# Where the softmax division happens in a top-32 attention with FFN, and how the weights reach their turned layout

## The chip, the cores and the metric

The kernel runs on one core of a Trainium2 chip. The metric is the time of one execution on the device, in microseconds. The time before is the median of three runs, 1543.8 us (1543.63 to 1544.71).

A core has five engines that run their own instruction streams in order: TensorE (PE; its weight loads are shown apart as PEld), VectorE (DVE), ScalarE (ACT), GpSimd (POOL) and SyncE (SP), which here only issues DMAs.

## The reference

```python
# q, k, v: (8, 8, 576, 64); w_in: (512, 2048); w_out: (2048, 512); all float32
scores = q @ k.T / 8
kth = 32nd largest of each row of scores
attn = exp(where(scores >= kth, scores, -1e9) - max)
attn = attn / (sum(attn) + 1e-9)
x = (attn @ v), heads put side by side: (4608, 512)
h = x @ w_in
out = (h - tanh(h)) @ w_out
```

So there is an attention in which each query keeps only its 32 best keys, and a feed-forward layer (FFN) on the result.

## The kernel before, in words

The work is cut into 144 steps. A step is one tile of 128 queries for one pair of heads (`hp`) of one batch `b`; z, the matrix of weights of a step, has 128 rows and 2 x 576 columns. Of the 576 queries of a batch four tiles of 128 are taken in pairs (`nq = 2`), and the last 64 of two head pairs make one step of remainders (`rem`, L-number names below are lines of the kernel). Batch 0 is treated in its own way (`pe`): its weights are turned by TensorE. The steps of batches 1 to 7 are 126: 56 pairs of query tiles and 14 remainders.

A step passes these stages, spread over five steps of a software pipeline written out by hand in `run`:

- `scores` (L237): matmuls into the one PSUM tile for scores, then a ScalarE copy to SBUF (L245).
- `search` (L267 to L278): VectorE finds the 32 largest of each row: a minimum and a maximum of the two halves (L267, L268), then four rounds of MAX8 and MATCH_REPLACE8. After each round, `between(i)` may place other VectorE work.
- `mask` (L294 to L314): GpSimd makes the threshold tb, ScalarE a penalty (L307), GpSimd subtracts it (L310).
- `expo` (L330): ScalarE takes the exponential and sums it; GpSimd adds the epsilon (L340) to give rd.
- `invert` (L345): for the last step of a pair, one VectorE reciprocal of the sums, rd.
- `turn_z` (L376): VectorE turns z within 32 x 32 blocks into zx. In the kernel before this stands in `between(0)`, after the first round of the search two steps later.
- `spread_keys` (L390): the blocks still have to move between the four groups of 32 partitions. Sixteen DMAs, one for each pair of groups, copy zx to et.
- `values` (L433): TensorE multiplies the turned weights with v. Because the weights have not been divided by their sums, the kernel repeats each 1/sum 64 times on GpSimd (L355, rx), turns this with a TensorE transpose (L441), copies product and turned sums out of PSUM (L445, xs), and multiplies the two on GpSimd (L457, L448) to give xT, the input of the FFN.
- `ffn_h` (L486, L498 to L500) and `ffn_o` (L507, L517, L519): the FFN. Its matmuls are the largest part of TensorE's work. They are not a stage of their own: `deal` hands them out in small items between the other instructions of a step, at a rate that `rate` plans from what is waiting and what is to come.

In step n of the loop, the instructions are placed in this order: values of step n-4 (if it is the last of its pair), mask of n-1, search of n with what `between` puts in, spread_keys of n-2, a share of the FFN items, scores of n+1, exponentials of n-1, and more FFN items. As every engine runs in order, this order is also what waits behind what.

Tiles that matter: zx has two buffers, et has one, z has two.

Of the kernel before, what the change touches and what calls it, by code (L numbers as in the profile page):

```python
# [8 lines left out]
AF = mybir.ActivationFunctionType  # L9
ALU = mybir.AluOpType  # L10
FP32 = mybir.dt.float32
# [37 lines left out]
def kernel(  # L49
# [9 lines left out]
    nc = tc.nc  # L59
    P = nc.NUM_PARTITIONS  # L60
# [4 lines left out]
    R = S - JP  # L65
    S2 = S // 2
    N = 2 * P
    CD = DM // P
    CF = DFF // P
    G = 32  # L70
    NG = P // G
    KC = 2 * S // P
    G = 32
    NG = P // G
    WJ = 4
    FJ = CF // WJ
    scale = 1.0 / float(D) ** 0.5
# [5 lines left out]
    def pool(name, bufs, **kw):  # L83
        return ctx.enter_context(tc.tile_pool(name=name, bufs=bufs, **kw))
# [10 lines left out]
    xrpool = pool("xr", 1)  # L95
    thpool = pool("th", 4)
    gpool = pool("g", 4)
    sc_ps = pool("sc_ps", 1, space=PS)
    zt_ps = pool("zt_ps", 2, space=PS)
    h_ps = pool("h_ps", 2, space=PS)  # L100

    ident = consts.tile([P, P], FP32, name="ident")
# [80 lines left out]
    def half(t):  # L183
        return slice(t * D, (t + 1) * D)
# [4 lines left out]
    def load_rows(name, b, hp, exact):  # L189
# [6 lines left out]
        src = {"k": k, "q": q}[name]  # L196
        for a in range(NG):
            h, d = 2 * hp + a // 2, a % 2 * G
            queue = nc.scalar if a and (name, b, hp, exact) == ("q", 0, 0, False) else nc.sync
            queue.dma_start(  # L200
                x[a * G : (a + 1) * G, :].rearrange("i (n d) -> i n d", d=G),
                src[b, h, :, d : d + G].rearrange("(n i) d -> i n d", i=G),
            )
# [22 lines left out]
    st = {}  # L226
# [97 lines left out]
    rds = {}  # L324
# [15 lines left out]
        nc.gpsimd.tensor_scalar(rd[:, g.i, :], den[:], EPS, None, ALU.add)  # L340

    def invert(n):
        if steps[n].last:
            rd = rds[n][:, 0 : steps[n].nq, :]
            nc.vector.reciprocal(rd, rd)  # L345

    rxs = {}

    def spread(n):

        if steps[n].last:
            rd = rds.pop(n)
            nq = steps[n].nq
            rx = rxs[n] = xpool.tile([P, 2, 2, D], FP32, tag="rx", name="rx")
            nc.gpsimd.tensor_copy(  # L355
                rx[:, 0:nq], rd[:, 0:nq].unsqueeze(3).to_broadcast([P, nq, 2, D])
            )
# [3 lines left out]
    def group(a):  # L361
        return slice(a * G, (a + 1) * G)

    def tiles(x, nq):

        x = x[:, 0 : nq * 2 * S]
        return x.rearrange("p (a k i j) -> p a k i j", a=NG, k=KC, j=G)

    def turn_z(n):


        g, z = steps[n], st.pop(n)["z"]
        if g.i == 0:
            last_zx[0] ^= 1
        zx = zxs[n] = zxs.pop(n - 1) if g.i else zx2[last_zx[0]]
        nc.vector.transpose(  # L376
            tiles(zx, g.nq)[:, :, :, g.i, :].rearrange("p c k j -> p k c j"),
            z[:].rearrange("p (k c j) -> p k c j", c=NG, j=G),
        )

    def spread_keys(n):


        zx = zxs.pop(n)
        rem = steps[n].rem
        et = ets[n] = et_rem if rem else etpool.tile([P, 4 * S], FP32, tag="et", name="et")
        w = steps[n].nq * S // 2
        for a in range(NG):
            for c in range(NG):
                nc.sync.dma_start(  # L390
                    et[group(c), a * w : (a + 1) * w], zx[group(a), c * w : (c + 1) * w]
                )

    def turn_pe(n):

# [9 lines left out]
        for k0 in range(0, KC, J):  # L405
# [10 lines left out]
            if k0:  # L416
                yield

    def values(n):

        g = steps[n]
        nq, u = g.nq, g.unit
        et = tiles(ets.pop(n), nq)
        rx = rxs.pop(n)
        w = nq * P
        av = zt_ps.tile([P, 2, N], FP32, tag="zt", name="av")
        for i in range(2 if g.rem else 1):
            cols = half(i) if g.rem else slice(0, w)
            es = et[:, 2 * i : 2 * i + 2] if g.rem else et
            hp = g.hp + i  # L430
            for c in range(J + 1):
                for t in range(2):
                    nc.tensor.matmul(  # L433
                        av[half(t), 0, cols],
                        vb[g.b, hp][:, t, c, :] if c < J else vr[g.b, hp][:, t, :],
                        es[:, :, (J + 1) * t + c if c < J else J].rearrange("p a i j -> p a (i j)"),
                        start=(c == 0),
                        stop=(c == J),
                    )
        for i in range(nq):  # L440
            nc.tensor.transpose(  # L441
                av[:, 1, 0:w].rearrange("p (a i j) -> p i a j", a=NG, i=nq)[:, i], rx[:, i].rearrange("p t d -> p (t d)"), ident[:]
            )
        xs = xrpool.tile([P, 2, N], FP32, tag="xs", name="xs")
        nc.scalar.copy(xs[:, :, 0:w], av[:, :, 0:w])  # L445
        if g.rem:
            for i in range(2):
                nc.gpsimd.tensor_tensor(  # L448
                    xt(u)[:, g.hp + i, g.col : g.col + R],
                    xs[:, 0, half(i)],  # L450
                    xs[:, 1, half(i)],
                    ALU.mult,
                )
        else:

            xv = xs[:, :, 0:w].rearrange("p s (a i j) -> p s i a j", a=NG, i=nq)
            nc.gpsimd.tensor_tensor(  # L457
                xt(u)[:, g.hp, g.col : g.col + w].rearrange("p (i a j) -> p i a j", a=NG, i=nq),
                xv[:, 0],
                xv[:, 1],  # L460
                ALU.mult,
            )
        if n in done:
            work.extend(ffn(u))

# [2 lines left out]
    def xt(u):  # L468
        if u.xT is None:
            p = xpool if u.tag == "xT" else xrpool  # L470
            u.xT = p.tile([P, CD, N], FP32, tag=u.tag, name=u.tag)
        return u.xT
# [48 lines left out]
    def ffn(u):  # L521

        nh = CF * u.n // (2 * P)
        for item in range(nh):
            f = (item + 1) * CF // nh - 1
            yield CD * (f // FJ + 1), u, lambda item=item: ffn_h(u, item)
        for i in range(len(u.blocks)):
            for part in range(CF // 2):
                yield CD * (WJ + part // 2 + 1), None, lambda i=i, part=part: ffn_o(u, i, part)
# [3 lines left out]
    steps, done, work = [], {}, []  # L533
# [36 lines left out]
    def run(exact):  # L570
# [9 lines left out]
        for i, (b, hp) in enumerate(pairs):  # L580
            n = next(n for n, g in enumerate(steps) if (g.b, g.hp) == (b, hp))
# [56 lines left out]
        def here(i):  # L638
            return 0 <= n + i < NS

        def between(i):
            for fn in at_round.pop((n, i), []):
                fn()
            if i == 0 and here(-2):
                invert(n - 2)
                if not steps[n - 2].pe:
                    turn_z(n - 2)


        ready, begun = {}, {}  # L650
# [31 lines left out]
        def deal(part):  # L682
            nonlocal credit
            credit += part * share
            while work and credit > 0 and work[0][0] <= usable:
                work.pop(0)[2]()
                credit -= 1
            credit = min(credit, 1.0)

        for n in range(-4, NS + 4):  # L690
            pe = here(-2) and steps[n - 2].pe
            if here(-3) and not steps[n - 3].pe:
                spread(n - 3)
            for m in (n - 4, n - 3):
                if 0 <= m < NS and steps[m].last and steps[m].lag == n - m:
                    values(m)
            share, usable = rate(), converted[0]
            if pe:
                w = turn_pe(n - 2)
                next(w)  # L700
            if here(-1):
                mask(n - 1, exact)
            if here(0):
                search(n, exact, between)
            elif here(-2):
                between(0)
            if here(-2) and not pe and steps[n - 2].last:
                spread_keys(n - 2)
            if pe:
                spread(n - 2)  # L710
            deal(0.0 if pe else 0.4)
            if here(1):
                scores(n + 1)
            if pe:
                next(w)
            if here(-1):
                expo(n - 1)
            deal(0.8 if pe else 0.2)
            if pe and steps[n - 2].last:
                values(n - 2)  # L720
            deal(0.0 if pe else 0.2)
            for fn in todo.pop(n, []):
                fn()
            deal(0.2)
# [4 lines left out]
    with tc.manual_schedule():  # L729
        run(False)  # L730
# [10 lines left out]
    with tc.If(again > 0):  # L741
        with tc.manual_schedule():
            run(True)
# [29 lines left out]
```

## Time and profile before

| | busy us | share of the span of 1542.8 us |
|---|---|---|
| TensorE, matmuls | 1440.7 | 93% |
| VectorE | 1347.2 | 87% |
| GpSimd | 940.8 | 61% |
| ScalarE | 883.9 | 57% |
| DMA queue q1 | - | 38.5% of 16 engines |

The rows that the change touches, from the groups of instructions (line, engine, count, busy time, mean of one):

| what | count | busy us | mean ns |
|---|---|---|---|
| L441 PE transposes of the repeated sums | 144 | 35.2 | 313 |
| L355 POOL repeats the sums | 84 | 30.8 | 367 |
| L445 ACT copies xs | 84 | 44.2 | 526 |
| L457 and L448 POOL multiply into xT | 100 | 56.8 | 695 and 321 |
| L345 DVE reciprocals | 84 | 14.0 | 167 |
| L376 DVE turns z | 126 instructions | 171.5 | 1361 |
| L390 DMAs zx to et | 1120 | 2.0 us each to landing | |

Busy time is the union of the intervals in which an engine ran such an instruction. Instructions of one engine overlap a little, so the mean of one times the count can exceed it. The idle time that a view shows ahead of an instruction is put down to the semaphore that came last.

### The profile page before, as it was taken

To read this page: it belongs to the slowest core of one execution; us is meant where nothing else is said; L and a number is where in the kernel's file an instruction comes from. 1 tells how busy PE (TensorE), PEld (TensorE's weight loads), DVE (VectorE), ACT (ScalarE), POOL (GpSimd) and SP (SyncE) were. 2 spreads that over 40 slices of the span, in tenths; PEclk is the share of its full clock that TensorE was granted. 3 is DMA by queue.
4 is the path that set the end of the run, shared out by engine and by line. 5 is a ranking of instruction groups with operands and counts; after the bars stand their busy time and mean duration, and the time that the engine had idled before them with its cause. 6 is when DMAs were issued, how large, how long until landed. Compare 5 with 4: busy or idle time off the path is not lost.

```text
span 1542.8 us, 25300 instructions
## 1 busy us (share of the span) xinstructions
PE 1440.7 (93%) x7428; PEld 912.1 (59%) x7428; DVE 1347.2 (87%) x3828; ACT 883.9 (57%) x1567; POOL 940.8 (61%) x1525
## 2 busy tenths in 40 slices
PE   2567899999999999999999999999999999999997
PEld 1355566465666666656566665656566665656673
DVE  6998899999999999999999999999999999997300
ACT  4887776566555565556555565556555565655320
POOL 2777677567665665756565675757565675746420
PEclk9887999999999999999999999999999999999999
DMA  9944113324533354234433354234433344322200
GB/s 241 360 169 168 50 32 76 78 71 102 112 86 80 76 112 101 70 79 95 106 87 79 77 110 103 70 78 96 102 89 79 77 103 109 78 67 58 73 8 16
DMA packets 258835, 147.42 MB, mean 96 GB/s; under 512 B 210048, under 2 KB 217216, under 8 KB 258688
## 3 DMA queue, kind: packets, MB, share of 16 engines
q1 hardware_dynamic: 256912, 145.49, 38.5%
q8 instruction: 62, 1.02, 0.3%
q14 instruction: 85, 0.70, 0.1%
q10 hardware_dynamic: 1776, 0.22, 0.1%
HBM read 61.85 MB, written 9.44 MB: 46 GB/s over the span
## 4 chain that ended last, share of the span: by engine, by line
PE 73%; DVE 10%; SPq 5%; ACT 4%; DMA 2%; issue 2%; POOL 2%; DVEq 0%; ACTq 0%; POOLq 0%
PE ops L507 28%; PE hps L486 26%; PE av L433 9%; PE scps L237 8%; SPq L390 3%; DVE m L275 2%; DVE ab L278 2%; PE av L441 2%; SPq L200 2%; DMA zx<-in_moe_w_in_dram 1%; DVE spare L376 1%; PE zt L409 1%; DVE ab L267 1%; DVE ab L270 1%; DVE ab L268 1%
## 5 line engine op out<-in xcount | busy, mean ns | idle before, releaser
L507 PE MATMUL ops<-w_out,g 128*128 128x512 f32 x1152 | 520.5, 598 | 0.0
L486 PE MATMUL hps<-xT,w_in 128*128 128x256 f32 (+1 forms) x2176 | 471.4, 372 | 1.2 <-POOL xT L457 1.2
L275 DVE MAX8 m<-ab 128x8 f32<-128x288 f32 (+1 forms) x1152 | 465.8, 447 | 0.0
L310 POOL TENSOR_TENSOR z<-sc,z 128x576 f32<-128x576 f32 x288 | 400.2, 1411 | 77.4 <-ACT z L307 77.4
L486 PEld LDWEIGHTS hps<-xT,w_in 128*128 128x128 f32 x2176 | 390.7, 193 | 73.9 <-issue 23.4
L278 DVE MATCH_REPLACE8 ab<-m,ab 128x288 f32<-128x288 f32 x864 | 377.3, 446 | 0.0
L507 PEld LDWEIGHTS ops<-w_out,g 128*128 128x128 f32 x1152 | 211.4, 191 | 244.8 <-issue 240.7
L307 ACT ACTIVATE z<-sc,tb 128x576 f32<-128x576 f32 x288 | 207.6, 769 | 153.1 <-POOL tb L294 153.1
L500 POOL TENSOR_TENSOR g<-g,th 128x512 f32<-128x512 f32 x144 | 183.7, 1276 | 123.5 <-ACT g L499 113.2
L330 ACT ACTIVATE z<-z,nb 128x576 f32<-128x576 f32 x288 | 221.6, 773 | 8.8 <-POOL z L310 8.7
L245 ACT COPY sc<-scps 128x1152 f32<-128x1152 f32 x144 | 160.9, 1117 | 108.5 <-PE scps L237 106.5
L237 PE MATMUL scps<-kT,qT 64*128 64x288 f32 (+1 forms) x1280 | 188.1, 445 | 31.7 <-DVE qT L222 28.1
L237 PEld LDWEIGHTS scps<-kT,qT 64*128 64x128 f32 (+1 forms) x1280 | 101.6, 184 | 120.5 <-issue 60.5
L267 DVE TENSOR_TENSOR ab<-scps,sc 128x576 f32<-128x576 f32 x144 | 108.0, 750 | 69.3 <-POOL bad L314 54.1
L433 PE MATMUL av<-et,vb 128*64 128x256 f32 (+1 forms) x1088 | 131.8, 378 | 37.2 <-ACT et L412 30.4
L457 POOL TENSOR_TENSOR xT<-xs 128x256 f32<-128x256 f32 (+1 forms) x68 | 47.2, 695 | 166.8 <-ACT xs L445 166.8
L498 ACT ACTIVATE th<-hps 128x512 f32<-128x512 f32 x144 | 85.4, 593 | 106.6 <-PE hps L486 104.1
L445 ACT COPY xs<-av 128x512 f32<-128x512 f32 (+1 forms) x84 | 44.2, 526 | 170.2 <-PE av L441 170.2
L433 PEld LDWEIGHTS av<-et,vb 128*64 128x64 f32 x1088 | 75.2, 139 | 98.6 <-ACT et L412 32.5
L340 POOL TENSOR_SCALAR rd<-den 128x2 f32<-128x2 f32 x144 | 33.4, 232 | 140.5 <-ACT z L330 98.2
L270 DVE MAX8 ab<-ab 128x8 f32<-128x288 f32 x288 | 116.9, 448 | 0.0
L268 DVE TENSOR_TENSOR ab<-scps,sc 128x576 f32<-128x576 f32 x144 | 107.8, 749 | 0.0
(67 smaller groups left out, 1253.9 us busy)
## 6 DMA issues: line engine op xcount, KB each, us to landing
et<-spare SPq DMA_DIRECT2D x448, 72.0 KB, 2.0
et<-zx SPq DMA_DIRECT2D x448, 72.0 KB, 2.0
kin<-in_k_dram SPq DMA_DIRECT2D x116, 72.0 KB, 2.4
vb<-in_v_dram SPq DMA_DIRECT2D x64, 128.0 KB, 2.5
out_dram<-ot SPq DMA_DIRECT2D x32, 256.0 KB, 2.2
qin<-in_q_dram SPq DMA_DIRECT2D x113, 72.0 KB, 2.3
w_out<-in_moe_w_in_dram SPq DMA_DIRECT2D x10, 512.0 KB, 5.3
w_out<-in_moe_w_in_dram SPq DMA_DIRECT2D x10, 511.5 KB, 6.1
```

Source lines behind the costliest of these rows:

```text
L237: nc.tensor.matmul(ps[rows, t, s, 0:S2], qT[g.b, g.hp + i][half(t), qs], kT[g.b, g.hp + i][half(t), ks], start=True, stop=True,)
L245: nc.scalar.copy(sc[:], ps[:, :, :, 0:S2])
L270: nc.vector.max(ab[:, t, S2 : S2 + 8], lo[:, t, :])
L275: nc.vector.max(m[:, t, m8], last[t] if i == rounds - 1 else cur[t])
L278: nc.vector.match_replace(nxt[t], m[:, t, m8], cur[t], NEG)
L307: nc.scalar.activation(zv[:, t, :], scf[:, t, :], AF.Relu, bias=tb[:, t : t + 1], scale=-BIG)
L310: nc.gpsimd.tensor_tensor(zv[:, t, :], scf[:, t, :], zv[:, t, :], ALU.subtract)
L330: nc.scalar.activation(x["zv"][:, t, :], x["zv"][:, t, :], AF.Exp, bias=x["nb"][:, t : t + 1], scale=scale, accum_out=den[:, t : t + 1],)
L433: nc.tensor.matmul(av[half(t), 0, cols], vb[g.b, hp][:, t, c, :] if c < J else vr[g.b, hp][:, t, :], es[:, :, (J + 1) * t + c if c < J els ...
L486: nc.tensor.matmul(cur[u][:, s : s + w], w_in[j][:, c, fo : fo + P], u.xT[:, c, 0:w], start=(c == 0), stop=(c == CD - 1),)
L500: nc.gpsimd.tensor_tensor(g, g, th[:], ALU.subtract)
L507: nc.tensor.matmul(cur[u][:], u.g[o // 1024][:, o % 1024 // 512, o % 512 : o % 512 + P], w_out[f // FJ][:, f % FJ, :], start=(f == 0), sto ...
```

## The change

The weights of batches 1 to 7 are divided by their sums before they are turned, by ScalarE (`divide`, two activations with a scale for each row). So the product with v is already the attention output: the repeated sums, their transposes, the copy xs and the GpSimd multiply are gone for these steps, and ScalarE copies the product from PSUM straight into xT. The reciprocal is now taken in each step, and the turning of z moves from after the first round of the search to after the third (`LATE = 2`), so that ScalarE has time for the division.

The sixteen copies between partition groups become one write of all of zx to a scratch tensor in DRAM (two buffers) and four reads, each of which collects the parts for one group of 32 partitions. The write of a pair is 1.18 MB, and the four reads are as much together.

```diff
+    LATE = 2
+    dpool = pool("d", 2, space=bass.MemoryType.DRAM)
     def invert(n):
-        if steps[n].last:
-            rd = rds[n][:, 0 : steps[n].nq, :]
+        g = steps[n]
+        if g.last and g.pe:
+            rd = rds[n][:, 0 : g.nq, :]
             nc.vector.reciprocal(rd, rd)
+        elif not g.pe:
+            rd = rds[n]
+            nc.vector.reciprocal(rd[:, g.i, :], rd[:, g.i, :])
+
+    def divide(n):
+
+        g = steps[n]
+        for t in range(2):
+            x = st[n]["zv"][:, t, :]
+            nc.scalar.activation(x, x, AF.Copy, scale=rds[n][:, g.i, t : t + 1])
+        if g.last:
+            rds.pop(n)
...
         w = steps[n].nq * S // 2
-        for a in range(NG):
-            for c in range(NG):
-                nc.sync.dma_start(
-                    et[group(c), a * w : (a + 1) * w], zx[group(a), c * w : (c + 1) * w]
-                )
+        there = dpool.tile([P, NG * w], FP32, tag=f"there{steps[n].nq}", name="there")
+        nc.sync.dma_start(there[:], zx[:, 0 : NG * w])
+        for c in range(NG):
+            nc.sync.dma_start(
+                et[group(c), 0 : NG * w].rearrange("i (a x) -> i a x", a=NG),
+                there[:, c * w : (c + 1) * w].rearrange("(a i) x -> i a x", a=NG),
+            )
...
-        for i in range(nq):
-            nc.tensor.transpose(
-                av[:, 1, 0:w].rearrange("p (a i j) -> p i a j", a=NG, i=nq)[:, i], rx[:, i].rearrange("p t d -> p (t d)"), ident[:]
-            )
-        xs = xrpool.tile([P, 2, N], FP32, tag="xs", name="xs")
-        nc.scalar.copy(xs[:, :, 0:w], av[:, :, 0:w])
+        if g.pe:
...
+        def put(dst, order, cols):
+            if g.pe:
+                nc.gpsimd.tensor_tensor(dst, order(xs[:, 0, cols]), order(xs[:, 1, cols]), ALU.mult)
+            else:
+                nc.scalar.copy(dst, order(av[:, 0, cols]))
...
             if i == 0 and here(-2):
                 invert(n - 2)
                 if not steps[n - 2].pe:
-                    turn_z(n - 2)
+                    divide(n - 2)
+            if i == LATE and here(-2) and not steps[n - 2].pe:
+                turn_z(n - 2)
...
         for n in range(-4, NS + 4):
             pe = here(-2) and steps[n - 2].pe
-            if here(-3) and not steps[n - 3].pe:
-                spread(n - 3)
```

More of the change, by code (lines that the diff above doesn't have):

```diff
@@ L72 @@
     KC = 2 * S // P
-    G = 32
-    NG = P // G
+    LATE = 2
     WJ = 4
@@ L417, in turn_pe, with in_order @@
                 yield
+    def in_order(x, nq):
+        return x.rearrange("p (a i j) -> p i a j", a=NG, i=nq)
     def values(n):
@@ L423, in values @@
         et = tiles(ets.pop(n), nq)
-        rx = rxs.pop(n)
         w = nq * P
@@ L439, in values @@
                     )
-        for i in range(nq):
-            nc.tensor.transpose(
-                av[:, 1, 0:w].rearrange("p (a i j) -> p i a j", a=NG, i=nq)[:, i], rx[:, i].rearrange("p t d -> p (t d)"), ident[:]
-            )
-        xs = xrpool.tile([P, 2, N], FP32, tag="xs", name="xs")
-        nc.scalar.copy(xs[:, :, 0:w], av[:, :, 0:w])
+        if g.pe:
+            rx = rxs.pop(n)
+            for i in range(nq):
+                nc.tensor.transpose(
+                    in_order(av[:, 1, 0:w], nq)[:, i], rx[:, i].rearrange("p t d -> p (t d)"), ident[:]
+                )
+            xs = xrpool.tile([P, 2, N], FP32, tag="xs", name="xs")
+            nc.scalar.copy(xs[:, :, 0:w], av[:, :, 0:w])
+        def put(dst, order, cols):
[3 more added lines that the diff above has]
+                nc.scalar.copy(dst, order(av[:, 0, cols]))
         if g.rem:
             for i in range(2):
[L448 to L453, printed above, removed]
-        else:
[L456 to L462, printed above, removed]
+                put(xt(u)[:, g.hp + i, g.col : g.col + R], lambda x: x, half(i))
+        else:
+            dst = xt(u)[:, g.hp, g.col : g.col + w].rearrange("p (i a j) -> p i a j", a=NG, i=nq)
+            put(dst, lambda x: in_order(x, nq), slice(0, w))
         if n in done:
@@ L706, in run @@
                 between(0)
+                between(LATE)
             if here(-2) and not pe and steps[n - 2].last:
```

## The prediction

> **What bounds the kernel now.** I read the page's busy shares first, then the windows view from 400 to 1400 us, the groups of instructions, the waits, and the timeline of three steps.
>
> ```profile
> PE 1440.7 (93%) x7428; PEld 912.1 (59%) x7428; DVE 1347.2 (87%) x3828; ACT 883.9 (57%) x1567; POOL 940.8 (61%) x1525
> ...
> 600.00:800.00 200.00, 199.40 (x989) 127.52 (x988) 190.22 (x542) 118.64 (x208) 131.61 (x214) 1.00 0.40 91
> 800.00:1000.00 200.00, 200.00 (x1034) 124.50 (x1033) 189.28 (x538) 114.11 (x203) 126.16 (x213) 1.00 0.37 84
> ```
>
> The columns of the windows are PE, PEld, DVE, ACT and POOL. From about 400 us TensorE has no gap (200.00 of 200 us, at full clock). [...]512-column passes follow each other at 0.43 us for runs of 16. VectorE is 95% busy and waits:
>
> ```profile
> DVE ab L267 <- POOL bad L314: 44.1, 51, 4.4
> DVE ab L267 <- ACT sc L245: 8.8, 9, 1.9
> ```
>
> The first line names GpSimd, but the timeline shows the true end of that wait:
>
> ```profile
> 801.02 0.76 DVE L267 TENSOR_TENSOR ab<-scps,sc 128x576 f32<-128x576 f32 x1 [0.80 <-POOL bad L314]
> 801.83 1.95 PE L433 MATMUL av<-et,vb 128*64 128x256 f32 x16
> 804.14 0.44 PE L441 MATMUL av<-ident,rx 128*128 128x128 f32 x2
> 804.41 3.60 PE L507 MATMUL ops<-w_out,g 128*128 128x512 f32 x8
> 804.65 0.17 DVE L345 RECIPROCAL rd<-rd 128x4 f32<-128x4 f32 x1
> 804.74 1.35 DVE L376 STREAM_TRANSPOSE spare<-z 128x1152 f32<-128x1152 f32 x1
> 806.15 10.28 SPq L390 DMA_DIRECT2D et<-spare  x16
> 806.33 1.44 ACT L307 ACTIVATE z<-sc,tb 128x576 f32<-128x576 f32 x2 [1.13 <-POOL tb L294]
> 807.94 1.24 PE L237 MATMUL scps<-kT,qT 64*128 64x288 f32 x8
> 809.28 1.12 ACT L245 COPY sc<-scps 128x1152 f32<-128x1152 f32 x1 [1.51 <-PE scps L237]
> 810.55 0.76 DVE L267 TENSOR_TENSOR ab<-scps,sc 128x576 f32<-128x576 f32 x1 [0.60 <-POOL bad L314]
> ```
>
> VectorE restarts 0.15 us after the score copy (L245) ends; GpSimd's work had ended long before. The copy waits for score matmuls, which stand in TensorE's order behind the values and dealt FFN matmuls. So TensorE sets the pace: 9.65 us a step (L267 starts at 636.50 and, 40 steps on, at 1022.47), while a VectorE step without a wait takes about 8.8 us. The exception is 250 to 400 us, where VectorE is 99% busy and TensorE 93 to 96%.
>
> [...]in the packet records 2304 B into 32 partitions takes 167 ns (13.8 GB/s per engine, 221 for 16), while 2048 B of an output write from all 128 partitions takes 85 ns (24 GB/s, 386 for 16).
>
> **The change, part by part.** Steps of batches 1 to 7 (126 of 144, 56 pairs of query tiles and 14 remainders) change; batch 0 keeps its way.
>
> *TensorE.* 126 transposes (L441) go. Busy time would say 126/144 of 35.2 us, 30.8 us, but matmuls overlap. By starts, two take 804.14 to 804.41, 0.27 us; one alone 0.17. Summed over the 126 from first start to next other start: 17.7 us. At the very end the FFN waits for the chain transposes, copy, multiply, xT; one scaled copy out of PSUM in place of that saves some 0.3 + 0.7 + 0.2 = 1.2 us. Nothing is added on TensorE. Full realization: 1543.8 - 18.9 = 1525.
>
> *VectorE.* A reciprocal per step instead of per pair: 56 more, 0.08 us from start to next start, 0.17 if nothing overlaps: 5 to 9 us. From 400 us on, VectorE's waits (44.1 + 8.8 us in 1000) hide it; in the 20 steps before, it is paid (1.6 us), and there the transposes' 2.8 us aren't gained either.
>
> *ScalarE.* 252 divisions of 576 elements, 0.77 us: 194 us more, two in each step (1.54 us). It loses the 512-wide xs copies (0.59) for 256-wide ones (about 0.38). Busy goes from 57% to about 70%. Do they delay anyone? They stand after L307 and before the FFN's tanh and the score copy. In an FFN-output step ScalarE idles 1.51 us just there (809.28 above), and L307 itself starts about 1.5 us sooner because its threshold no longer queues on GpSimd behind the xT multiply (L457). In the other kind, with tanh and copy between, TensorE's first half of FFN work (3.6 us after the values) covers L307 plus divisions (0.4 + 1.44 + 1.54). I cost them at nothing for the score copy, but the transpose of z (L376) now waits for them: VectorE reaches it 6.8 us after L267, divisions end about 6.6 to 7.5 us after it, so 0 to 0.7 us of wait in some steps, inside VectorE's slack of 0.5 us a step.
>
> *GpSimd* loses rx and the multiplies, about 31 + 57 us less the part of batch 0; it is off the path.
>
> *The way through DRAM.* This is the risk. The transpose moves two rounds later: it ended 5.05 us after L267, now at 6.8 + 1.37 = 8.2, so 3.15 later. Before, 16 copies took 9.5 to 10.3 us to issue and 2.0 to land: 12 us. Now one write of 1.18 MB, then, after its landing, four reads. The write: 73.7 KB per engine at 24 GB/s is 3.05 us, plus 1.4 (a 256 KB output lands in 2.05, of which 0.68 is data): 4.45 (estimate). The reads: 32 packets per engine at 167 ns is 5.3 us, at 90 ns (what 4096 B in 159 ns scales to) 2.9[...]. Sum 9.4 to 11.8. I take the upper end, since the reads fill 32 partitions each. The values matmuls come 14.9 to 16.2 us after the old transposes' end (820.98 - 806.1), so the data must land 3.15 + 11.8 = 14.95 after it: just in time.
>
> As a loop over four steps: landing; values to VectorE's restart 8.72 - 0.27 = 8.45; a VectorE step 8.87; 8.2 to the end of the transposes; 0.4 for key and query transposes, shared out: 26.0 + L. TensorE's own four steps are 38.6 - 0.56 = 38.0, so L may be 12.0 before the loop binds. Behind these reads on SyncE's queue stand k, q, v loads and output stores; the write's landing blocks them 4.5 us, but the queue is then free after 7 us instead of 10.
>
> *Sum.* 1525, plus 4.4 us for the VectorE-bound stretch, plus about 4 us of late landings and late divisions (L is within 0.3 us of the bound, steps differ by up to 1 us, and only some of that is elastic): 1533.
>
> **Rivals.** (a) Everything hides, L near 10: 1525 + 4 = 1529, down to 1524. For it: the loop's margin would be 2 us. (b) The DRAM round trip sets the pace: L of 12.5 makes the loop 38.5/4 = 9.63, no gain; L of 13.0 gives 9.75, 0.1 us a step more than before over 126 steps, and the early stretch some 5 us: 1543.8 + 13 + 5, near 1560, slower. For it: [...]write traffic to DRAM that the trace shows only in 256 KB pieces, and other loads on the same engines; against: 16 issues of 0.6 us go. (c) Divisions hold VectorE: if the transposes wait 0.7 us in half of the steps with slack already spent, some 126 x 0.5 x 0.25 = 16 us come back and the time stays at about 1543. For it: ScalarE runs in order and its tanh waits for TensorE (L498, 104 us in all). Against: idle time before L245.
>
> **How the numbers follow.** My forecast 0.40 (1530 to 1540), (a) 0.25, (c) and mild forms of (b) 0.13, (b) 0.22. Faster by over 0.2% (under 1540.7) is the first two and a little: 0.65; same 0.12; slower 0.23. The range reaches from (a) to most of (b): 1524 to 1553.
>
> **What would show it.** Right: L441 down to 18 or so transposes, TensorE still over 99% busy from 450 us, step 9.5 us, DRAM write landing about 4.5 us and last read about 11.8 us after the write's issue. Wrong: "PE av <- DMA et" waits of over 20 us (rival b), VectorE waiting on z L356 before its transposes for over 40 us (rival c), or an L of 10 with waits none (a).

## The result and the profile after

The changed kernel takes 1565.7 us against 1544.3 us: 1.0137 times as long (95% interval 1.0122 to 1.0152). The forecast was 1533, faster; it is slower by 21 us. (The time before is here the median of four runs; 1543.8 was that of the first three.)

The page of the changed kernel, in the same columns as before: busy time and share of each engine, two groups of instructions with the idle time ahead of them, and the DMAs with their size and time to landing.

```profile
PE 1436.2 (92%) x7302; PEld 912.5 (58%) x7302; DVE 1353.4 (86%) x3884; ACT 1029.3 (66%) x1833; POOL 869.6 (56%) x1371
...
L356 ACT ACTIVATE z<-z,rd 128x576 f32<-128x576 f32 x252 | 180.1, 763 | 12.9 <-DVE rd L349 12.3
...
L389 DVE STREAM_TRANSPOSE zx<-z 128x1152 f32<-128x1152 f32 x63 | 86.6, 1374 | 35.1 <-ACT z L356 34.9
...
et<-there SPq DMA_DIRECT2D x224, 288.0 KB, 5.3
there<-spare SPq DMA_DIRECT2D x28, 1152.0 KB, 4.2
```

The parts cost what was put down for them: a division 763 ns (0.77 us was put down; L307, an activation of the same shape, has a mean of 769 ns before), the write to DRAM 4.2 us. What is new is idle time. VectorE now waits for the division ahead of L389, the transposes of z; both halves of that group (zx and spare, the two buffers; the remainders' et lies in spare too) together wait 67.8 us, where before it was 4.1. TensorE has lost its closed row, as the windows view shows (columns PE, PEld, DVE, ACT, POOL, clock, DMA share, GB/s):

```profile
600.00:800.00 200.00, 196.27 (x988) 125.45 (x987) 189.95 (x550) 139.53 (x250) 117.16 (x188) 1.00 0.57 147
800.00:1000.00 200.00, 194.66 (x991) 122.65 (x991) 185.58 (x532) 135.32 (x241) 113.67 (x183) 0.99 0.56 145
```

From 400 to 1400 us TensorE was busy 997.1 us before and 975.3 now. The waits view of that stretch (us in total, times, longest) names what it stands for: the values matmuls (L452 now) and the data that they need. Their two PE lines are 23.0 of the 24.7 us that TensorE is idle; before, its waits for these data came to 1.5 us.

```profile
DVE zx L389 <- ACT z L356: 21.4, 23, 3.2
DVE spare L389 <- ACT z L356: 21.0, 22, 3.7
PE av L452 <- DMA et<-there: 18.7, 20, 2.9
PE av L452 <- issue: 4.3, 5, 1.6
```

Two steps of the timeline, with other rows left out, show both waits:

```profile
800.70 1.37 DVE L389 STREAM_TRANSPOSE zx<-z 128x1152 f32<-128x1152 f32 x1
...
802.10 0.34 SPq L402 DMA_DIRECT2D there<-zx  x1
...
803.39 0.76 DVE L267 TENSOR_TENSOR ab<-scps,sc 128x576 f32<-128x576 f32 x1 [0.60 <-ACT sc L245]
...
806.33 2.10 SPq L404 DMA_DIRECT2D et<-there  x4
...
806.96 1.27 POOL L517 TENSOR_TENSOR g<-g,th 128x512 f32<-128x512 f32 x1 [1.83 <-ACT g L516]
807.02 0.16 DVE L349 RECIPROCAL rd<-rd 128x2 f32<-128x2 f32 x1
808.22 0.56 POOL L294 TENSOR_SCALAR tb<-m 128x1 f32<-128x1 f32 x2
...
808.55 1.44 ACT L307 ACTIVATE z<-sc,tb 128x576 f32<-128x576 f32 x2 [1.67 <-POOL tb L294]
...
809.89 1.43 ACT L356 ACTIVATE z<-z,rd 128x576 f32<-128x576 f32 x2
...
811.35 1.38 DVE L389 STREAM_TRANSPOSE spare<-z 128x1152 f32<-128x1152 f32 x1 [1.04 <-ACT z L356]
...
814.43 1.95 PE L452 MATMUL av<-et,vb 128*64 128x256 f32 x16 [0.43 <-DMA et<-there]
...
820.37 1.24 PE L237 MATMUL scps<-kT,qT 64*128 64x288 f32 x8
821.54 7.13 PE L524 MATMUL ops<-w_out,g 128*128 128x512 f32 x16
...
821.66 1.12 ACT L245 COPY sc<-scps 128x1152 f32<-128x1152 f32 x1 [1.77 <-PE scps L237]
...
822.88 0.76 DVE L267 TENSOR_TENSOR ab<-scps,sc 128x576 f32<-128x576 f32 x1 [0.61 <-ACT sc L245]
```

The reciprocal is there at 807.2, but the division begins at 809.89, because L307 stands ahead of it on ScalarE, L307 waits for the threshold, and the threshold queues on GpSimd behind the FFN's subtraction. And the values matmuls at 814.43 wait for a landing: their transposes ended at 802.07, the write went out at 802.10 and the reads from 806.33. The scores behind them, and so VectorE's restart at 822.88, are late by as much, 0.43 us here and up to 2.9 elsewhere. The transposes at 811.35 belong to a later pair; their lateness goes into VectorE's step at once.

From the starts in the traces: from the end of a pair's transposes to its values matmuls it is 15.2 us in the median before. After, it is 12.16 us with a least of 11.88, and 50 of the 56 pairs lie under 12.9. The last copy landed 11.8 us after the transposes before, the last read lands 12.0 us after them now (medians). So before, the data lay there for 3.2 us until TensorE came to them; now the values matmuls start as the data land. The step (starts of L267, steps 42 to 138) went from 9.64 to 9.83 us, and steps 20 to 42, where VectorE had been the bound, from 9.18 to 9.67.

### The profile page after: what moved, and what is told of

Read it like the earlier page. It is cut to its first block, busy times and chain, and to the rows that moved or that the text cites. A ratio compares the mean times of both kernels' runs of the same rounds, so it can differ in the third digit from the quotient of the medians.

```text
span 1565.0 us, 24008 instructions
## 1 busy us (share of the span) xinstructions
PE 1436.2 (92%) x7302; PEld 912.5 (58%) x7302; DVE 1353.4 (86%) x3884; ACT 1029.3 (66%) x1833; POOL 869.6 (56%) x1371
## 4 chain that ended last, share of the span: by engine, by line
PE 45%; DMA 19%; DVE 16%; ACT 9%; issue 4%; SPq 4%; POOL 3%; DVEq 0%; ACTq 0%; POOLq 0%
PE ops L524 16%; PE hps L503 15%; DMA et<-there 11%; PE av L452 8%; DMA there<-zx 5%; DVE m L275 5%; PE scps L237 4%; DVE ab L278 4%; DMA there<-spare 3%; ACT z L307 2%; ACT z L356 2%; SPq L404 2%; POOL g L517 1%; SPq L200 1%; DVE ab L270 1%
## 5 line engine op out<-in xcount | busy, mean ns | idle before, releaser
L517 POOL TENSOR_TENSOR g<-g,th 128x512 f32<-128x512 f32 x144 | 183.5, 1275 | 152.1 <-ACT g L516 147.0
L307 ACT ACTIVATE z<-sc,tb 128x576 f32<-128x576 f32 x288 | 207.6, 770 | 73.8 <-POOL tb L294 73.3
L452 PE MATMUL av<-et,vb 128*64 128x256 f32 (+1 forms) x1088 | 136.4, 387 | 70.9 <-DMA et<-there 33.3
L356 ACT ACTIVATE z<-z,rd 128x576 f32<-128x576 f32 x252 | 180.1, 763 | 12.9 <-DVE rd L349 12.3
L452 PEld LDWEIGHTS av<-et,vb 128*64 128x64 f32 x1088 | 83.7, 142 | 129.8 <-issue 66.9
L267 DVE TENSOR_TENSOR ab<-scps,sc 128x576 f32<-128x576 f32 x144 | 107.0, 743 | 31.2 <-ACT sc L245 24.3
L389 DVE STREAM_TRANSPOSE zx<-z 128x1152 f32<-128x1152 f32 x63 | 86.6, 1374 | 35.1 <-ACT z L356 34.9
L472 ACT COPY xT<-av 128x256 f32<-128x256 f32 x56 | 20.8, 372 | 145.7 <-PE av L452 145.7
```

The source lines that it names most:

```text
L307: nc.scalar.activation(zv[:, t, :], scf[:, t, :], AF.Relu, bias=tb[:, t : t + 1], scale=-BIG)
L356: nc.scalar.activation(x, x, AF.Copy, scale=rds[n][:, g.i, t : t + 1])
L452: nc.tensor.matmul(av[half(t), 0, cols], vb[g.b, hp][:, t, c, :] if c < J else vr[g.b, hp][:, t, :], es[:, :, (J + 1) * t + c if c < J els ...
L517: nc.gpsimd.tensor_tensor(g, g, th[:], ALU.subtract)
```

## The experiments

The first four take the change apart. L-numbers in the lines shown are those of each run's own kernel, so e1, e2, e3, e4 and e9 to e11 differ by a few from the changed kernel. Each ratio is to the kernel before as it ran beside that run (medians of 1542.8 to 1546.4 us). Steps 42 to 138 in the column "step"; "waits" is VectorE's idle time ahead of its transposes of z.

| run | us | ratio to before (95%) | step us | waits us |
|---|---|---|---|---|
| changed kernel | 1565.7 | 1.0137 (1.0122 to 1.0152) | 9.83 | 67.8 |
| e1 DRAM alone | 1541.7 | 0.9981 (0.9973 to 0.9990) | 9.63 | 4.1 |
| e2 division alone | 1587.1 | 1.0279 (1.0257 to 1.0301) | 9.97 | 82.7 |
| e3 no division | 1549.4 | 1.0035 (1.0021 to 1.0049) | 9.69 | 0 |
| e4 no division, first round | 1527.1 | 0.9892 (0.9874 to 0.9909) | 9.53 | 0 |
| e5 scores first | 1533.9 | 0.9940 (0.9924 to 0.9957) | 9.57 | 52.7 |
| e6 mask behind | 1552.2 | 1.0055 (1.0039 to 1.0072) | 9.69 | 16.2 |
| e7 both | 1549.6 | 1.0044 (1.0027 to 1.0061) | 9.63 | 10.8 |
| e8 LATE = 1 | 1569.7 | 1.0155 (1.0128 to 1.0182) | 9.83 | 93.4 |
| e9 flags first | 1537.6 | 0.9966 (0.9952 to 0.9979) | 9.54 | 16.0 |
| e10 reciprocal first | 1529.3 | 0.9909 (0.9893 to 0.9924) | 9.53 | 11.1 |
| e11 flags, from batch 1 | 1527.8 | 0.9884 (0.9866 to 0.9902) | 9.54 | 16.0 |

**e1: the way through DRAM alone,** in the kernel before.

```diff
+    dpool = pool("d", 2, space=bass.MemoryType.DRAM)
...
-        for a in range(NG):
-            for c in range(NG):
-                nc.sync.dma_start(
-                    et[group(c), a * w : (a + 1) * w], zx[group(a), c * w : (c + 1) * w]
-                )
+        there = dpool.tile([P, NG * w], FP32, tag=f"there{steps[n].nq}", name="there")
+        nc.sync.dma_start(there[:], zx[:, 0 : NG * w])
+        for c in range(NG):
+            nc.sync.dma_start(
+                et[group(c), 0 : NG * w].rearrange("i (a x) -> i a x", a=NG),
+                there[:, c * w : (c + 1) * w].rearrange("(a i) x -> i a x", a=NG),
+            )
```

> The kernel before with one part of the change: the way through DRAM in place of the sixteen copies. Theory A (a loop over four steps through the late transposes, the landing and the values matmuls sets the pace of the changed kernel): here the transposes still end 5.05 us after L267, so the loop is 12.1 + 8.72 + 8.87 + 5.05 + 0.4 = 35.1 us for four steps, under TensorE's 38.6, and the time stays at that of the kernel before, 1544 +- 5. Theory B (the round trip through DRAM is the fault by itself): the 21 us come with this part, and without the 17.7 us saved on TensorE it is slower than the changed kernel: 1566 to 1585.

Measured 1541.7 us, a little faster than before. Theory B, the round trip as the fault by itself, falls. The step hardly changes, 9.63 against 9.64; in the traces 2.5 us of the gain lie behind step 138.

**e2: the division alone,** the changed kernel with the sixteen copies (the diff of e1 turned round).

> The changed kernel with the sixteen copies of the kernel before in place of the way through DRAM. Theory A: sixteen copies take as long to land as the round trip (9.5 to 10.3 us of issue + 2.0), so nothing is gained: 1560 to 1570. Theory B: the loss goes with the round trip and TensorE's saving stays: 1525 to 1540.

1587.1 us: theory B falls again, but theory A's 1560 to 1570 was missed too. From the transposes' end to the values matmuls it is 12.1 us, as in the changed kernel; so for pairs the two ways are alike. What the waits view of this run shows in addition is waiting for the remainders' copies (those into spare; et<-spare are pairs):

```profile
PE av L449 <- DMA spare<-spare: 10.9, 5, 3.0
PE av L449 <- DMA et<-spare: 8.1, 8, 1.8
PE av L449 <- DMA spare<-zx: 7.0, 4, 2.2
```

A remainder needs sixteen issues as a pair does, behind those of the pair on SyncE's queue, and its second block of values matmuls needs the last of them. From the end of a remainder's transposes to the search that its values matmuls hold up it is 22.9 us here and 21.6 in the changed kernel (means from step 42 on); over 14 remainders that is about 19 us, an estimate from these starts. That this makes up the 21 us over the changed kernel is likely, but no run took it apart.

**e3 and e4: without the two activations of `divide`** (the outputs of batches 1 to 7 stay undivided); in e4 the transposes are also back after the first round.

```diff
-        for t in range(2):
-            x = st[n]["zv"][:, t, :]
-            nc.scalar.activation(x, x, AF.Copy, scale=rds[n][:, g.i, t : t + 1])
# and in e4
-    LATE = 2
+    LATE = 0
...
                 between(0)
-                between(LATE)
```

> The changed kernel without the two activations of divide (the outputs of batches 1 to 7 are left undivided); transposes still after the third round. Theory A with the waits for the division as one half of the loss: VectorE's 68 us of waits before its transposes vanish, the loop is 12.1 + 8.45 + 8.87 + 8.2 + 0.4 = 38.0 us for four steps, 9.5 a step in place of 9.825: 1533 to 1545. Theory C (the late landing alone is the fault, the waits for the division are elastic): 1558 to 1566.

> As the run before, and the transposes back after the first round (the outputs of batches 1 to 7 are left undivided). Theory A: the loop falls to 34.7 us for four steps, TensorE is the bound again and keeps its saving of 17.7 us and 1.2 at the end: 1523 to 1530. If TensorE's transposes cost nothing in truth (they overlap), 1540 to 1545.

e3 took 1549.4 us, 16.3 less than the changed kernel: the waits for the division are real, not elastic, so theory C falls; but it stayed 4 us over theory A's upper end. e4 took 1527.1, as expected, with TensorE closed again (e3 first, then e4):

```profile
400.00:1400.00 1000.00, 987.52 (x5009) 618.16 (x5007) 946.66 (x2725) 558.55 (x1023) 575.83 (x924) 1.00 0.58 149
400.00:1400.00 1000.00, 997.96 (x5092) 624.15 (x5090) 957.37 (x2763) 568.35 (x1039) 586.15 (x938) 1.00 0.58 150
```

So a saving is there: 1544.3 - 1527.1 = 17.2 us, of which the way through DRAM alone gives 2.6 (e1). And the 38.6 us that the changed kernel loses over e4 are, taken apart in this order, 16.3 with the division and 22.3 with the later place of the transposes.

**e5: the values matmuls behind the next scores,** in the changed kernel, for the steps of batches 1 to 7.

```diff
             for m in (n - 4, n - 3):
-                if 0 <= m < NS and steps[m].last and steps[m].lag == n - m:
+                if 0 <= m < NS and steps[m].last and steps[m].lag == n - m and steps[m].pe:
                     values(m)
...
             if here(1):
                 scores(n + 1)
+            for m in (n - 4, n - 3):
+                if 0 <= m < NS and steps[m].last and steps[m].lag == n - m and not steps[m].pe:
+                    values(m)
```

> The changed kernel with one move: in steps of batches 1 to 7 the values matmuls stand behind the next step's score matmuls instead of ahead of them, so that the wait for the landing no longer stands between VectorE and its next scores. Theory A (the loop through landing and scores): the loop loses the score path, about 12.1 + 12 + 8.2 = 32 us for four steps, under TensorE's 38.0; VectorE's waits for the division stay but are elastic: 1526 to 1536. Theory C (the waits for the division alone set the pace, some 0.55 us a step): 1545 to 1560.

1533.9 us: 32 us come back (30 by the ratios) by a move that shortens no instruction, with the division and the late transposes as they were. VectorE still waits 52.7 us for the division, and that is now largely elastic; before L267 it waits 4.8 us from step 42 on, against 24.2 in the changed kernel. It is not wholly elastic: TensorE now waits for VectorE to read the one PSUM tile for scores (L268), while its wait for the landing is gone.

```profile
PE scps L237 <- DVE ab L268: 10.8, 7, 3.7
PE av L452 <- DMA et<-there: 0.4, 1, 0.4
```

**e6: the mask behind the division.** **e7: both moves.**

```diff
-            if here(-1):
+            late = here(-2) and not steps[n - 2].pe
+            if here(-1) and not late:
                 mask(n - 1, exact)
...
                     divide(n - 2)
+                    if here(-1):
+                        mask(n - 1, exact)
```

> The changed kernel with one move: the mask of the step before (L307 and GpSimd's part) is placed behind the division, so that ScalarE divides as soon as the reciprocal is there. Theory A: VectorE's waits before its transposes fall from 68 us to under 20, and the loop with its landing of 12.1 us stays as without the division, 9.69 us a step: 1545 to 1555. If the waits for the division come from elsewhere than the order on ScalarE: 1562 to 1568.

> Both moves together. Theory A: neither the landing nor the division is in a loop that binds, TensorE sets the pace with its 17.7 us fewer: 1524 to 1531. If the 145 us more that ScalarE works bind by themselves: 1540 or more.

e6 came out as expected: the waits fall to 16.2 us, the step to the 9.69 of e3. ScalarE's order is what made VectorE wait. From 400 to 1400 us little is left of it, while the wait for the landing stays in part:

```profile
PE av L452 <- DMA et<-there: 9.7, 16, 2.5
DVE spare L389 <- ACT z L356: 1.0, 1, 1.0
DVE zx L389 <- ACT z L356: 0.7, 1, 0.7
```

e7, the edits of e5 and e6 together, missed by 19 us. Its timeline shows a new loop (other rows left out):

```profile
304.41 0.76 DVE L267 TENSOR_TENSOR ab<-scps,sc 128x576 f32<-128x576 f32 x1 [0.52 <-POOL bad L314]
...
308.04 0.15 DVE L349 RECIPROCAL rd<-rd 128x2 f32<-128x2 f32 x1
...
308.29 1.44 ACT L356 ACTIVATE z<-z,rd 128x576 f32<-128x576 f32 x2 [3.57 <-DVE rd L349]
309.63 1.43 ACT L307 ACTIVATE z<-sc,tb 128x576 f32<-128x576 f32 x2
...
310.47 2.79 POOL L310 TENSOR_TENSOR z<-sc,z 128x576 f32<-128x576 f32 x2 [4.57 <-ACT z L307]
...
313.25 0.58 POOL L314 TENSOR_SCALAR bad<-ab,tb 128x1 uint8<-128x1 f32 x2
...
313.86 0.76 DVE L267 TENSOR_TENSOR ab<-scps,sc 128x576 f32<-128x576 f32 x1 [0.53 <-POOL bad L314]
```

This time the named releaser is the true one: the flags (L314) end at 313.83 and VectorE restarts at 313.86. They are the last readers of the search buffer ab, which has two copies, and moving the mask put them behind reciprocal, division, penalty and subtraction: 9.45 us from search to search. This holds 69 of the 118 steps from 20 to 137. It is no longer than TensorE's mean step in e4, 9.53, but the steps are unequal: in e4 they take from 8.8 to 10.5 us (steps 42 to 138). A floor of 9.45 takes away the short ones and leaves the long ones, so it can cost time all the same; the mean of e7 is 9.63, and e9 and e10 below show that this loop is what held it.

**e8: LATE = 1,** the transposes after the second round.

```diff
-    LATE = 2
+    LATE = 1
```

> The changed kernel with LATE = 1: the transposes stand after the second round, 1.55 us sooner, while the division ends when it did. Theory A (end of the division sets the end of the transposes, and VectorE's wait lengthens its own step, which stands in the loop): waits before the transposes grow by about 1.2 us a step, to over 180 us, and the time to 1570 to 1600. Theory D (the place of the transposes sets the landing): 1.55 us off the loop, 1545 to 1555.

1569.7 us with 93.4 us of waits. Theory D falls: the transposes that complete a pair do end sooner, 7.5 us after L267 in the mean where it was 8.7, but nothing is gained. From the values matmuls to the search that they hold up it is now 9.6 us, where it was 8.6: VectorE, with its waits for the division, comes late of itself. The time is just under theory A's lower edge and its waits are half of those expected. Before L267 VectorE's wait fell from 24.2 us to 1.6 (from step 42 on), so the wait mostly changed its place.

**e9 to e11: the new loop of e7 cut.** e9 puts the flags ahead of GpSimd's subtractions, e10 puts the reciprocal ahead of the first round instead, e11 is e9 with the flags moved only from batch 1 on. All three have both moves of e7.

```diff
# e9, in mask: the loop that writes bad now stands ahead of
         z = zpool.tile([P, 2 * S], FP32, tag="z", name="z")
# e10
+        between(-1)
         rounds = TOP // 8
...
-            if i == 0 and here(-2):
+            if here(-2) and i == (0 if steps[n - 2].pe else -1):
                 invert(n - 2)
```

> Both moves as in e7, and GpSimd's two flag instructions (L314, bad) placed ahead of its subtractions instead of behind them. Theory E (in e7 the next search waits for those flags, since they are the last readers of its buffer ab and now stand behind reciprocal, division, penalty and subtraction, a chain of 9.45 us a step): the wait of VectorE before L267 goes, TensorE is the bound with its saving: 1524 to 1531. If e7 is held by ScalarE's work or by anything else: 1545 to 1550.

> Both moves as in e7, and the reciprocal ahead of the first round of the search instead of behind it, which takes about 1.7 us off the same chain. Theory E: 9.45 - 1.7 = 7.75 us a step, below TensorE's 9.5: 1524 to 1532. If e7 is held by anything else: 1545 to 1550.

> As e9, but the flags stand ahead of GpSimd's subtractions only from batch 1 on. Theory F (e9 fell short of 1531 because the earlier flags delay batch 0: its step 18 began at 228.94 us in place of 221.75 in e7): about 7 us come back, 1528 to 1533. If e9's rest comes from later steps: 1536 to 1539.

e10 took 1529.3 us, as expected. e9's 1537.6 was 7 us over. e11, which differs from it in batch 0 alone, took 1527.8 us, just under its range, so what e9 lacked was lost there. The size of that loss is known less well: the medians differ by 9.8 us (12.7 by the ratios), while step 18 begins at 228.94 us in e9's trace and at 224.72 in e11's, and among the kernels with the same batch 0 this start goes from 221.75 (e7) to 226.81 (e2). e11 is 0.9884 of before: it does all of the reference's work and equals e4, which leaves the division out. Its waits view from 400 to 1400 us has next to nothing of the two waits of the changed kernel:

```profile
DVE spare L395 <- ACT z L362: 4.2, 4, 1.3
...
DVE zx L395 <- ACT z L362: 1.6, 3, 0.8
PE av L458 <- DMA et<-there: 0.2, 1, 0.2
```

## Why the prediction was wrong

**What bounds the kernel before: right.** e4 takes away TensorE's 126 transposes and adds no wait, and TensorE stays busy 997.96 of 1000 us while the time falls by 17.2 us. It takes away work of GpSimd and ScalarE too, which no run parts from this; they were busy 61% and 57% of the span before.

**TensorE's term: right within a few us.** 17.7 + 1.2 us were put down; e4 gains 17.2, of which the way through DRAM, put at no gain, accounts for 2.6. So the busy time of 30.8 us would have been the wrong price.

**VectorE's added reciprocals: right in size.** There are 56 more, and all of them together are busy 21.7 us against 14.0; 5 to 9 were put down.

**ScalarE, "inside VectorE's slack of 0.5 us a step": this step failed.** The wait itself was seen, 0 to 0.7 us in some steps. It measured 67.8 us in 58 places, up to 3.7 us from 400 to 1400 us and 6.3 at the end, and e3 shows that it costs 16.3. Two parts of the step failed. First, L307 was to start about 1.5 us sooner where the xT multiply leaves GpSimd. In these steps it starts 4.4 us after L267 (median) where it was 5.4, which is 1.0. And in half of all steps (62 of 124) the threshold now starts right behind the FFN's subtraction L517, as at 808.22 above; 49 us of the waits lie in these. Of the 53 steps that never had the multiply, 24 are among them; there L307 starts 5.2 us after L267, where it was 2.8. Second, the slack was that of a VectorE that waits for TensorE; in the changed kernel VectorE's wait before L267 is down to 24.2 us from 61.2 (from step 42 on).

**The way through DRAM, "just in time": the price was right, the loop around it failed.** The estimate was 9.4 to 11.8 us, and 11.8 was used. The last read landed 11.93 us after the write's issue in the median: 4.17 for the write, where 4.45 was put down, and 7.67 from the first read's issue to the last landing, where 7.2 was: 5.3 for the packets and 1.9, an assumption of the author's, for the rest. In the trace of the changed kernel the packets of a pair's four reads fill 5.94 of the 7.67 us, from 0.95 to 6.89 us after the first issue (medians), and 1.73 lie outside them. From the landing to the values matmuls the author assumed 0.1; it is 0.14 in the median. Up to the values matmuls it is 12.16 us. The loop was said to bind from 12.0 on; with 12.16 its sum is 38.1 us for four steps, 9.53 a step, no more than TensorE's own. e3, which has this loop without waits for the division, runs at 9.69: the sum was 0.6 us short for four steps. The starts of e3 (steps 42 to 138) show two things that it leaves out. Around a step of remainders, a landing holds up the very step whose transposes complete the next pair or remainder. So it is for 23 of the 41 pairs there; VectorE's extra step drops out, and the loop is 8.2 + 12.1 + 8.5 = 28.8 us for three steps, 9.6 a step. And the mean of the pairs is 12.6 us from transposes to values, not the median's 12.3, since single ones take up to 14.6. How the 0.6 us divides between these two is open. The waits for the division add the rest up to 9.83. Instead of the forecast's 4 us of late landings and late divisions, the changed kernel loses 38.6 us over e4.

**The VectorE-bound stretch: the term was about right, but a loss was left out.** 4.4 us were put down for reciprocals that are paid and a saving that is not gained. e4 has both, and takes 217.8 us from step 18 to 42, against 218.4 before. The changed kernel takes 229.1: some 11 of the 38.6 us are waits in this stretch, for which the sum has nothing.

**The rivals.** The signs of (b) and (c) both came: 33.3 us of "PE av <- DMA et" over the whole span, 67.8 us of waits for the division. Each came in a mild form and both together, while they were given a chance of 0.35 as alternatives; and the range ended at 1553, short of the 1560 that (b) itself gives. The DRAM trip was blamed in (b) for what belongs to the place of the transposes: e1 has the trip and loses nothing.

The case as a whole: before, the transfer and the values matmuls stood in a loop with 3.5 us to spare in four steps (35.1 against 38.6, from the expectation of e1). The later place of the transposes took 3.1 of them (their end went from 5.05 us after L267 to 8.2) and the shorter work of TensorE 0.6, so that nothing was left, and the division then made that end later still (8.7 in the mean). e5 and e11 show that order, not work, was at fault.

## What to carry to other kernels

A saving on the bounding engine is kept only if every loop of waits through the steps stays shorter than the new, smaller pace: e4, its loop put at 34.7 us for four steps, kept it, and e3, its loop put at 38.1, as long as TensorE's own four steps, lost it. Add up each loop in the order in which the engines will run, also at the places where the steps follow each other in another way (here around the remainders), and take a margin of 1 or 2% as none: in e3 the sum was 0.6 us short in 38.8, and where steps are unequal, a loop as long as the mean step can already cost time, as in e7 (9.45 us against e4's mean of 9.53). When work is moved later in a step, look at what stands behind the waiting instruction on each engine: putting the next scores ahead of the waiting matmuls gave back about 30 us at no cost, and moving the mask created a new wait through a buffer's last reader. Where a named releaser had long ended, look further; where its end and the restart are 0.03 us apart, as in e7, believe it.

## What the runs showed that was not expected

One 1.18 MB write to DRAM and four reads brought the data to the values matmuls as soon as sixteen direct copies between partitions, in about 12 us (the last copy landed 11.8 us after the transposes in the kernel before, the last read 12.0 in the changed one), though every byte makes two trips (221.6 MB are moved in the whole run, 147.4 before), and alone (e1) they were 0.2% faster. The DMA view of the changed kernel from 800 to 840 us, GB/s in 40 slices of 1 us:

```profile
GB/s 0 0 74 406 406 311 0 85 288 210 205 230 182 220 63 0 0 0 0 0 0 0 295 442 424 18 28 247 210 187 242 203 226 100 0 0 16 0 0 0
```

The write moves at about 406 GB/s and the reads into 32 partitions at about 210, half of it. In the packet records, 2304 B of such a read take 184 ns (median of the 56 pairs), 9216 B of the write 352. Reading from DRAM is not slow as such: loads that are mostly weights, into all 128 partitions, move at 349 to 421 GB/s in the kernel before (29 to 69 us). The pieces there are longer too, 4096 bytes (159 ns) against 2304, and no run took apart which of the two makes the reads slower.
